# Preparing the coefficients of a long convolution: its products put behind the phase pieces, one input split over two queues, part of the scaling on ScalarE

## The chip, the cores and the metric

The kernel runs on one core of one Trainium2 chip. The metric is the device time of one execution in microseconds (us). The kernel before took 429.4 us, the median of three runs (428.68, 429.65 and 429.40). Its profile is of one further execution, which took 426.76 us.

## The reference

Two independent parts are computed and put side by side. Part A is a windowed attention (2048 tokens, 32 heads of 20, a window of 8 keys with a distance of 2). Part B is a state-space convolution over 2048 steps in 640 channels with 192 complex states for each; the change touches only its preparation:

```python
dt = jnp.exp(log_dt)[:, None]
A = A_re + 1j * A_im
Bc = B_re + 1j * B_im
Cc = C_re + 1j * C_im
logdA = dt * A
dB = dt * Bc
P = jnp.exp(logdA[:, :, None] * l[None, None, :])       # l = 0 .. 2047
K = jnp.einsum("dn,dnl,dn->dl", Cc, P, dB).real
...                                                     # y = the causal convolution of u with K, by FFT
y = y + u * Dskip[None, None, :]
return jnp.concatenate([a, b], axis=-1)
```

So three things are needed for each channel and state: the decay dt·A_re, the phase dt·A_im and the coefficient C·dt·B.

## The kernel before, in words

The 640 channels lie as 128 partitions by 5 chunks (NCH = 5). `partB_prep` loads the parameters and holds a helper `fill(c0, c1, between)`, called first for chunk 0 alone and then for chunks 1 to 4 together. For its chunks it does, in the order of its text:

- **decays** (L161 to L165): TensorE multiplies B_A_re by a diagonal of dt (tile DG) into PSUM (tile `ps_tr`) and ScalarE copies the result to `alpha`, a part of the tile LPC;
- **phase** (L182 to L194): VectorE works out dt·A_im in turns, once by itself and once times 32, each reduced to its fraction, and splits each fraction into three bf16 **pieces** hi, mid and lo (`pieces`, L168 to L174);
- **moves** (`move`, L176 to L180): twelve small DMAs carry the pieces into the tile LPC in the layout that TensorE wants, half of them issued by SyncE (SP) and half by GpSimd (POOL). The `between` of the second call also issues the loads of the tile U;
- **coefficients** (L196 to L202): for the real and the imaginary part two VectorE products p1 and p2 of B with C, their difference or sum, and one scaling by dt·4/3 for each chunk (L202), which writes the tile CN.

`B["coefficients"](c, ...)` (L204 to L211) then has TensorE transpose CN of one chunk against the constants `mix` into four PSUM tiles `ps_tr`, and ScalarE copies these to the tile cT. `psum_p` gives `ps_tr` two buffers.

`exps_chunk` (L216) lets ScalarE write powers of the decay (tile R, 45 exponentials for each chunk). `trig_half(c, h)` (L236) lets TensorE expand LPC into phases (`ps_ph`, three PSUM buffers) and ScalarE take the sine of them into the tiles TA (four activations) and TX (four activations) for one half h of a chunk; there is one buffer of TX, so the second half's TX waits until VectorE has read the first's. `small_half` (L275) is VectorE work: PG from R and TA, then Q from PG and cT, then the two X tiles from R and TX. `y_form` (L306) and `kgen_unit` (L316) form the convolution kernel from these, and everything after it (forward transform, products, inverse transform, attention) follows in `body`.

`body` (L696) writes the start in this order: chunk 0 with `fill(0, 1)`, `coefficients(0)`, constants, `exps_chunk` of chunk 0, `trig_half(0, 0)`, `fill(1, 5)`, then a loop over the chunks. The Tile framework's scheduler decides the order in which the instructions stand in each engine's queue; the engines work their queues strictly in that order. Only instructions passed through `late` (`keep_in_program_order`) are held in the order of the text, among them the DMAs. B_C_re is loaded by four DMAs on the SP queue behind the four of B_B_re; B_C_im is loaded on the POOL queue.

Some buffers matter later. The tiles of the preparation lie in the same memory that the tiles PG, Q, X and Y of the main loop use afterwards, so the first writers of those wait for the last readers of the preparation's tiles.

Of the kernel before, what the change touches and what calls it, by code (L numbers as in the profile page):

```python
# [10 lines left out]
A = mybir.AluOpType  # L11
# [83 lines left out]
def partB_prep(tc, pools, prm):  # L95
# [21 lines left out]
    def load(nm):  # L117
        nat[nm] = (pl if nm == "B_A_re" else pd).tile([128, NCH, 192], bf16, name=nm, tag=nm)
        src = prm[nm].rearrange("(g u t c) n -> u g t (c n)", g=4, u=4, t=8)
        for u in range(4):  # L120
            queue = {"B_A_re": (nc.scalar, nc.sync)[u % 2], "B_A_im": nc.gpsimd, "B_B_im": nc.gpsimd, "B_C_im": nc.gpsimd}.get(nm, nc.sync)
            late(queue.dma_start(out=nat[nm][32 * u:32 * u + 32].rearrange("p c n -> p (c n)"), in_=src[u]))

    load("B_A_re")
# [10 lines left out]
    late(nc.scalar.activation(out=dtb[:], in_=ldt[:], func=ACT.Exp))  # L135
    dtc = pl.tile([128, NCH], f32, name="dtc")
    V.tensor_copy(out=dtc[:], in_=dtb[:])
    id32 = cpool.tile([128, 32], bf16, name="id32", tag="id32")
    for u in range(4):
        V.tensor_copy(out=id32[32 * u:32 * u + 32, :], in_=ident[32 * u:32 * u + 32, 32 * u:32 * u + 32])  # L140
# [6 lines left out]
    def transposed(u, parts):  # L147

        for (o, sT, rhs, first) in parts:
            MM(o[..., 0:32], lhsT=sT[:, 0:128], rhs=rhs, start=first, stop=True, skip_group_check=True, tile_position=(32 * u, 0))  # L150
        for (o, sT, rhs, first) in parts:
            for h in range(2):
                MM(o[64 * h:64 * h + 64, ..., 32:48], lhsT=sT[:, 128:192], rhs=rhs[..., 16 * h:16 * h + 16], start=False, stop=True, skip_group_check=True, tile_position=(32 * u, 64 * h))

    def fill(c0, c1, between):
        n = c1 - c0
        cs = range(c0, c1)
        fl = lambda t: t.rearrange("p c w -> p (c w)")
        T = lambda nm, dt_, tag=None, pool=pd: pool.tile([128, n, 192], dt_, name=nm, tag=f"{tag or nm}_{n}")

        for u in range(4):  # L161
            sl = slice(32 * u, 32 * u + 32)
            ps = pspool.tile([128, NCH, UW], f32, name="ps_tr", tag="bank")
            transposed(u, [(ps[:, i], nat["B_A_re"][sl, c], DG[sl, c, :], i == 0) for i, c in enumerate(cs)])
            nc.scalar.copy(out=alpha[:, c0:c1, u, :], in_=ps[:, 0:n])  # L165
        parts = [(pd if n == 1 else ph).tile([128, 2, n * 192], bf16, name=nm, tag=f"{nm}_{n}") for nm in ("hi", "mid", "lo")]

        def pieces(b, f):  # L168
# [24 lines left out]
        pieces(0, g1)  # L193
        pieces(1, g32)  # L194
        move(between)
        for ri, (n1, n2, n3, n4, op) in enumerate((("B_B_re", "B_C_re", "B_B_im", "B_C_im", A.subtract), ("B_B_re", "B_C_im", "B_B_im", "B_C_re", A.add))):  # L196
            p1, p2 = T(f"p1{ri}", f32, "fp1"), T(f"p2{ri}", f32, "fp2")
            V.tensor_tensor(out=fl(p1), in0=fl(nat[n1][:, c0:c1]), in1=fl(nat[n2][:, c0:c1]), op=A.mult)
            V.tensor_tensor(out=fl(p2), in0=fl(nat[n3][:, c0:c1]), in1=fl(nat[n4][:, c0:c1]), op=A.mult)
            V.tensor_tensor(out=fl(p1), in0=fl(p1), in1=fl(p2), op=op)  # L200
            for i, c in enumerate(cs):
                V.tensor_scalar(out=CN[:, c, ri], in0=p1[:, i], scalar1=dtc[:, c:c + 1], scalar2=4.0 / 3.0, op0=A.mult, op1=A.mult)  # L202

    def coefficients(c, pool):  # L204
        for u in range(4):
# [4 lines left out]
                           (ps[:, 3:4], re, mix[sl, 7:8], False), (ps[:, 2:3], im, mix[sl, 8:9], False)])  # L210
            nc.scalar.copy(out=cT[:, c, u // 2, :, 12 * (u % 2):12 * (u % 2) + 12, :].rearrange("p w q f -> p w (q f)"), in_=ps[:])  # L211

    return dict(CF1=CF1, CF32=CF32, LP=LP, alpha=alpha, cT=cT, coefficients=coefficients), fill


def exps_chunk(tc, pools, B, c):  # L216
# [479 lines left out]
def body(tc, ctx, pools, prm, B_u, B_Dskip, Sd, Zd, UDd, A_x, A_wqkv, A_wo, out_a, out_b):  # L696
# [14 lines left out]
    with tc.tile_pool(name="prep_l", bufs=1) as pl, tc.tile_pool(name="prep_d", bufs=1) as pd, tc.tile_pool(name="prep_g", bufs=1) as pg, tc.tile_pool(name="prep_h", bufs=1) as ph, tc.tile_pool(name="psum_p", bufs=2, space=bass.MemoryType.PSUM) as psp:  # L711
        pools.update(prep_l=pl, prep_d=pd, prep_h=ph)
        pg.tile([128, GAP], bf16, name="gap")
        B, fill = partB_prep(tc, dict(pools, psum=psp), prm)
        fill(0, 1, lambda u: None)
        B["coefficients"](0, psp)
        Dn = pl.tile([128, 160], bf16, name="Dn")
        dsrc = B_Dskip.rearrange("(g ch) -> g ch", g=4)
        late = tc.keep_in_program_order
        late(nc.sync.dma_start(out=BD[:].rearrange("p a b n -> p (a b n)"), in_=inline(nc, cn["BD"], "c_BD")))  # L720
        late(nc.sync.dma_start(out=EA[:].rearrange("p a n -> p (a n)"), in_=inline(nc, cn["EA"], "c_EA")))
        late(nc.sync.dma_start(out=T2[:].rearrange("p a n -> p (a n)"), in_=inline(nc, cn["T2"], "c_T2")))
# [5 lines left out]
        fill(1, NCH, lambda g: late(nc.sync.dma_start(out=U[32 * g:32 * g + 32], in_=usrc[g])))  # L728
# [226 lines left out]
```

## Time and profile before

| | before |
|---|---|
| time, median of 3 runs | 429.4 us (428.68 to 429.65) |
| the profiled execution's own time | 426.76 us |
| its span in the trace | 425.0 us |
| granted TensorE clock, mean | 0.94 of full speed |
| HBM read, written | 28.08 MB, 18.35 MB |
| start of the first PG on VectorE | 31.47 us |
| start of the second half's TX on ScalarE | 41.14 us |

The span is the time from the first to the last event of the trace; what lies around it is 426.76 - 425.0 = 1.76 us. Times in a timeline are counted from the start of the span. In a timeline row stand the start, the duration of the row's instructions together, the engine, the line, the operation, what is written and read, the count, and in brackets the idle time of the engine just before and what ended it. Instructions of an engine are pipelined, so the next can start a little before the last has ended: the step from start to start is what a queue pays. PE is TensorE's matmul, PEld its weight load, DVE is VectorE, ACT is ScalarE, POOL is GpSimd and SPq is SyncE's DMA issue.

### The profile page before, as it was taken

To read this page: it belongs to the slowest core of one execution; us is meant where nothing else is said; L and a number is where in the kernel's file an instruction comes from. 1 tells how busy PE (TensorE), PEld (TensorE's weight loads), DVE (VectorE), ACT (ScalarE), POOL (GpSimd) and SP (SyncE) were. 2 spreads that over 40 slices of the span, in tenths; PEclk is the share of its full clock that TensorE was granted. 3 is DMA by queue.
4 is the path that set the end of the run, shared out by engine and by line. 5 is a ranking of instruction groups with operands and counts; after the bars stand their busy time and mean duration, and the time that the engine had idled before them with its cause. 6 is when DMAs were issued, how large, how long until landed. Compare 5 with 4: busy or idle time off the path is not lost. (4 is left out here: it accounts for less than half of the span.)

```text
span 425.0 us, 18968 instructions
## 1 busy us (share of the span) xinstructions
PE 351.9 (83%) x8693; PEld 261.5 (62%) x8693; DVE 379.0 (89%) x353; ACT 312.0 (73%) x574; POOL 39.1 (9%) x83
## 2 busy tenths in 40 slices
PE   1294769979996989969897799999799989879795
PEld 0183668867974778758785677545545666445353
DVE  7899997998997999999996989855987999999671
ACT  3984989789999999979998684433757545656552
POOL 7430000000000000000010000100000300502120
PEclk9998668999999898978997899999999999999899
DMA  5579103073233402334079942600040553887542
GB/s 148 166 174 201 25 3 126 29 244 83 102 128 127 100 29 103 143 110 102 29 274 239 217 102 93 231 2 3 2 100 2 175 114 108 239 218 203 158 127 93
DMA packets 45280, 51.76 MB, mean 122 GB/s; under 512 B 31392, under 2 KB 39136, under 8 KB 42512
## 3 DMA queue, kind: packets, MB, share of 16 engines
q1 hardware_dynamic: 41664, 41.47, 35.8%
q0 software_dynamic: 3392, 8.95, 7.2%
q8 instruction: 68, 1.11, 1.1%
q10 hardware_dynamic: 144, 0.12, 0.1%
q14 instruction: 12, 0.10, 0.1%
HBM read 28.08 MB, written 18.35 MB: 109 GB/s over the span
## 5 line engine op out<-in xcount | busy, mean ns | idle before, releaser
L312 DVE TENSOR_TENSOR Y<-PG 128x3072 bf16<-128x3072 bf16 x60 | 103.1, 1752 | 5.6 <-PE ps_k L330 5.5
L258 PE MATMUL ps_ph<-LPC 128*64 128x256 bf16 x400 | 43.7, 317 | 16.0 <-DMA LPC<-lo 8.7
L325 PE MATMUL ps_k<-Y,X 128*32 128x64 bf16 x1920 | 46.9, 239 | 8.6 <-issue 4.7
L330 PE MATMUL ps_k<-Y,X 64*32 64x64 bf16 x1920 | 44.6, 233 | 3.8 <-issue 3.8
L353 ACT CAST Sg<-ps_f 128x1024 bf16<-128x1024 f32 x40 | 37.7, 1038 | 7.7 <-PE ps_f L352 7.7
L325 PEld LDWEIGHTS <-X 128*32 128x32 bf16 x1920 | 32.2, 117 | 17.9 <-issue 9.7
L232 ACT ACTIVATE R<-LPC 128x192 bf16<-128x192 f32 x155 | 41.9, 387 | 0.0
L345 ACT CAST A<-ps_f 128x1024 bf16<-128x1024 f32 x40 | 38.0, 1045 | 2.6 <-PE ps_f L344 2.6
L330 PEld LDWEIGHTS <-X 64*32 64x32 bf16 x1920 | 30.0, 113 | 13.2 <-issue 5.3
L352 PE MATMUL ps_f<-A,T 128*64 128x128 bf16 x640 | 28.8, 265 | 10.8 <-ACT A L345 9.8
L282 DVE TENSOR_TENSOR X<-R,TX 128x1536 bf16<-128x1536 bf16 x40 | 37.2, 951 | 0.0
L258 PEld LDWEIGHTS <-LPC 128*64 128x64 bf16 x400 | 21.7, 122 | 21.7 <-issue 16.9
L266 ACT ACTIVATE TX<-ps_ph 128x768 bf16<-128x768 int16 x40 | 29.8, 837 | 6.9 <-DVE X L282 5.2
L352 PEld LDWEIGHTS <-T 128*64 128x64 bf16 x640 | 27.1, 141 | 12.4 <-issue 12.1
L618 DVE TENSOR_TENSOR prod<-v,atp 128x2048 bf16<-128x2048 bf16 (+2 forms) x32 | 30.8, 1020 | 3.5 <-PE ps_o L429 3.5
L266 ACT ACTIVATE TA<-ps_ph 128x768 bf16<-128x768 int16 x40 | 30.1, 818 | 1.4 <-PE ps_ph L262 1.4
L262 PE MATMUL ps_ph<-LPC 128*64 128x128 bf16 x400 | 29.0, 240 | 0.0
L429 PE MATMUL ps_op<-wo,o 128*128 128x320 bf16 x160 | 24.9, 307 | 1.6 <-ACT ob L430 0.9
L262 PEld LDWEIGHTS <-LPC 128*64 128x64 bf16 x400 | 24.5, 126 | 0.8
L367 DVE TENSOR_TENSOR P<-P,Sg 128x4096 bf16<-128x4096 bf16 x10 | 22.9, 2285 | 2.0 <-DMA P<-Sdram 1.6
L531 DVE TENSOR_TENSOR prod<-qT,kT 128x1024 bf16<-128x1024 bf16 (+1 forms) x16 | 23.0, 1483 | 0.5 <-ACT qT L499 0.5
L282 DVE TENSOR_TENSOR PG<-R,TA 128x3072 bf16<-128x3072 bf16 x10 | 17.5, 1752 | 6.5 <-ACT TA L266 6.5
(132 smaller groups left out, 663.9 us busy)
## 6 DMA issues: line engine op xcount, KB each, us to landing
Sdram<-Sg SPq DMA_DIRECT2D x5, 1024.0 KB
P<-Sdram SPq DMA_DIRECT2D x5, 1024.0 KB
P<-Sdram SPq DMA_DIRECT2D x10, 512.0 KB
Zdram<-Z SPq DMA_DIRECT2D x5, 1024.0 KB
Z<-Zdram SPq DMA_DIRECT2D x30, 128.0 KB
U<-in_B_u_dram SPq DMA_DIRECT2D x4, 640.0 KB
UDdram<-UD SPq DMA_DIRECT2D x10, 256.0 KB
out_dram<-ysb SPq DMA_DIRECT2D x32, 80.0 KB
```

The costliest lines, as they stand in the source:

```text
L232: nc.scalar.activation(out=RX[:, :, e - 16, :], in_=src, func=ACT.Exp, scale=m)
L258: MM(o[64 * hh:64 * hh + 64, :, 0:8], lhsT=L[:, 64 * hh:64 * hh + 64], rhs=rhs, start=first, stop=last, skip_group_check=True, tile_positi ...
L262: MM(o[64 * hh:64 * hh + 64, :, 8:12], lhsT=L[:, 128:192], rhs=rhs[:, :, 16 * hh:16 * hh + 16], start=False, stop=last, skip_group_check=T ...
L266: last = nc.scalar.activation(out=dst, in_=words.rearrange("p b (q e f) -> p b q (e f)", e=8, f=4), func=ACT.Sin, scale=PI_LO / 32768.0)
L282: TT = lambda o, a, b, op: V.tensor_tensor(out=o, in0=a, in1=b, op=op)
L312: nc.vector.tensor_tensor(out=Y[:].rearrange("p q (b a) f -> p q b a f", a=8), in0=fa, in1=gb, op=A.mult)
L325: MM(ps[32 * g:32 * g + 32, t], lhsT=X[:, q, k, :, f], rhs=Ys[k][:, q, :, f], start=(t == 0 and k == 0), stop=False, tile_position=(0, 32 ...
L330: MM(ps[32 * g:32 * g + 32, t], lhsT=X[hb, q, k, :, f], rhs=Ys[k][hb, q, :, f], start=False, stop=(k == 2), tile_position=(64 * (g // 2), ...
L345: nc.scalar.copy(out=A1[:, :, 32 * b:32 * b + 32].rearrange("p k (j g) -> p k j g", g=4), in_=ps[:].rearrange("p j k g -> p k j g"))
L352: last = MM(ps[sl, kk], lhsT=C["T2"][:, 8 * b + kk, sl], rhs=A1[:, 8 * b + kk, :], start=(kk % 4 == 0), stop=True, skip_group_check=True, ...
L353: nc.scalar.copy(out=Sg[:, :, 8 * b:8 * b + 8, :], in_=ps[:].rearrange("p k (j g) -> p j k g", g=4))
L618: ins = nc.vector.tensor_tensor(out=p2.rearrange("p (d i) -> p d i", i=ni), in0=self.v2[:, 4 * j0:4 * j0 + 4 * nj, off:off + ni], in1=at[: ...
```

## The change

- `fill` loses its first and its last part. The decays become `decays(c0, c1)`, the coefficients become `weights(c0, c1)`. `body` now calls, in this order: decays of chunk 0, `fill` of chunk 0, constants, exponentials, `trig_half(0, 0)`, `fill` of chunks 1 to 4, `weights` of chunk 0, `coefficients(0)`, decays of chunks 1 to 4, `weights` of chunks 1 to 4.
- B_C_re is loaded half on POOL (ahead of B_C_im there) and half on SP.
- A new tile `dts` holds dt·4/3, so that the scaling has one factor in place of two.
- The scaling of the real part of chunks 1 to 4 becomes four ScalarE activations (Copy with a scale); the other six scalings stay on VectorE.
- The products of the imaginary part no longer share buffers with those of the real part, but use those of the phase's tiles (tags fa and fb).

```diff
-            queue = {"B_A_re": (nc.scalar, nc.sync)[u % 2], "B_A_im": nc.gpsimd, "B_B_im": nc.gpsimd, "B_C_im": nc.gpsimd}.get(nm, nc.sync)
+            queue = {"B_A_re": (nc.scalar, nc.sync)[u % 2], "B_A_im": nc.gpsimd, "B_B_im": nc.gpsimd, "B_C_im": nc.gpsimd, "B_C_re": (nc.gpsimd, nc.sync)[u // 2]}.get(nm, nc.sync)
...
     V.tensor_copy(out=dtc[:], in_=dtb[:])
+    dts = pools["fft"].tile([128, NCH], f32, name="dts")
+    V.tensor_scalar(out=dts[:], in0=dtc[:], scalar1=4.0 / 3.0, scalar2=None, op0=A.mult)
...
+    def decays(c0, c1):
+        for u in range(4):
+            sl = slice(32 * u, 32 * u + 32)
+            ps = pspool.tile([128, NCH, UW], f32, name="ps_tr", tag="bank")
+            transposed(u, [(ps[:, i], nat["B_A_re"][sl, c], DG[sl, c, :], i == 0) for i, c in enumerate(range(c0, c1))])
+            nc.scalar.copy(out=alpha[:, c0:c1, u, :], in_=ps[:, 0:c1 - c0])
...
-        for u in range(4):
-            sl = slice(32 * u, 32 * u + 32)
-            ps = pspool.tile([128, NCH, UW], f32, name="ps_tr", tag="bank")
-            transposed(u, [(ps[:, i], nat["B_A_re"][sl, c], DG[sl, c, :], i == 0) for i, c in enumerate(cs)])
-            nc.scalar.copy(out=alpha[:, c0:c1, u, :], in_=ps[:, 0:n])
...
         move(between)
+
+    def weights(c0, c1):
+        n = c1 - c0
+        fl = lambda t: t.rearrange("p c w -> p (c w)")
+        T = lambda nm, dt_, tag: pd.tile([128, n, 192], dt_, name=nm, tag=f"{tag}_{n}")
         for ri, (n1, n2, n3, n4, op) in enumerate((("B_B_re", "B_C_re", "B_B_im", "B_C_im", A.subtract), ("B_B_re", "B_C_im", "B_B_im", "B_C_re", A.add))):
-            p1, p2 = T(f"p1{ri}", f32, "fp1"), T(f"p2{ri}", f32, "fp2")
+            p1, p2 = T(f"p1{ri}", f32, ("fp1", "fa")[ri]), T(f"p2{ri}", f32, ("fp2", "fb")[ri])
...
-            for i, c in enumerate(cs):
-                V.tensor_scalar(out=CN[:, c, ri], in0=p1[:, i], scalar1=dtc[:, c:c + 1], scalar2=4.0 / 3.0, op0=A.mult, op1=A.mult)
+            for i, c in enumerate(range(c0, c1)):
+                if n == 1 or ri == 1:
+                    V.tensor_scalar(out=CN[:, c, ri], in0=p1[:, i], scalar1=dts[:, c:c + 1], scalar2=None, op0=A.mult)
+                else:
+                    nc.scalar.activation(out=CN[:, c, ri], in_=p1[:, i], func=ACT.Copy, scale=dts[:, c:c + 1])
...
+        B["decays"](0, 1)
         fill(0, 1, lambda u: None)
-        B["coefficients"](0, psp)
...
         fill(1, NCH, lambda g: late(nc.sync.dma_start(out=U[32 * g:32 * g + 32], in_=usrc[g])))
+        B["weights"](0, 1)
+        B["coefficients"](0, psp)
+        B["decays"](1, NCH)
+        B["weights"](1, NCH)
```

In the built program the change moves instructions only in the first part of each queue; from the first PG on, VectorE's queue is the same as before.

More of the change, by code (lines that the diff above doesn't have):

```diff
@@ L211, in coefficients @@
             nc.scalar.copy(out=cT[:, c, u // 2, :, 12 * (u % 2):12 * (u % 2) + 12, :].rearrange("p w q f -> p w (q f)"), in_=ps[:])
-    return dict(CF1=CF1, CF32=CF32, LP=LP, alpha=alpha, cT=cT, coefficients=coefficients), fill
+    return dict(CF1=CF1, CF32=CF32, LP=LP, alpha=alpha, cT=cT, decays=decays, weights=weights, coefficients=coefficients), fill
 def exps_chunk(tc, pools, B, c):
```

## Prediction

> **What bounds the kernel now.** I read the page's totals first, then busy time by stage, then VectorE's waits, then the timeline of the first 42 us.
>
> ```profile
> span 425.0 us, 18968 instructions
> PE 351.9 (83%) x8693; PEld 261.5 (62%) x8693; DVE 379.0 (89%) x353; ACT 312.0 (73%) x574; POOL 39.1 (9%) x83
> ```
>
> VectorE is the fullest engine, but the change touches only the start, so the start must be read by itself. This is the windows view; its columns are the window, its length, the busy time (and count) of PE, PEld, DVE, ACT and POOL, the granted clock, the DMA share and GB/s.
>
> ```profile
> 0.00:20.00 20.00, 2.27 (x20) 1.51 (x22) 15.79 (x44) 12.67 (x48) 12.59 (x27) 1.00 0.53 141
> 20.00:31.50 11.50, 11.47 (x164) 9.63 (x162) 11.39 (x22) 9.83 (x21) 3.83 (x7) 1.00 0.79 199
> 31.50:50.00 18.50, 10.50 (x349) 8.50 (x345) 18.50 (x17) 12.53 (x30) 0.00 (x0) 0.73 0.84 134
> 50.00:74.00 24.00, 19.93 (x520) 17.36 (x522) 21.86 (x19) 22.68 (x52) 0.61 (x2) 0.78 0.15 57
> ```
>
> From 20 to 50 us VectorE is busy for 29.89 of 30 us, while ScalarE has 7.6 us free. From 50 to 74 us ScalarE is the fuller one (22.68 of 24). So VectorE sets the pace of the start, if it is also what ScalarE's stretch waits for. Among VectorE's waits only one in the preparation is over 1 us once its work has begun:
>
> ```profile
> DVE p L198 <- DMA LPC<-hi: 1.8, 1, 1.8
> ```
>
> The timeline shows where it lies and what hangs on the end of the preparation:
>
> ```profile
> 14.37 0.95 DVE L172 TENSOR_TENSOR m<-tg,hi 128x768 f32<-128x768 f32 x1
> ...
> 17.14 0.36 DVE L198 TENSOR_TENSOR p<-B_B_re,B_C_re 128x192 f32<-128x192 bf16 x1 [1.82 <-DMA LPC<-hi]
> ...
> 26.56 1.07 DVE L202 TENSOR_SCALAR CN<-p,dtc 128x192 bf16<-128x192 f32 x4
> ...
> 27.55 0.94 DVE L199 TENSOR_TENSOR p<-B_B_im,B_C_re 128x768 f32<-128x768 bf16 x1
> ...
> 31.47 1.75 DVE L282 TENSOR_TENSOR PG<-R,TA 128x3072 bf16<-128x3072 bf16 x1
> ...
> 34.01 1.75 DVE L282 TENSOR_TENSOR Q<-PG,cT 128x3072 bf16<-128x3072 bf16 x1
> ...
> 39.22 1.82 DVE L282 TENSOR_TENSOR X<-R,TX 128x1536 bf16<-128x1536 bf16 x2
> ...
> 41.14 2.92 ACT L266 ACTIVATE TX<-ps_ph 128x768 bf16<-128x768 int16 x4 [5.15 <-DVE X L282]
> ```
>
> The instruction at 17.14 reads only B_B_re and B_C_re, so it waited for the last B_C_re load; the row's "LPC<-hi" is a later load of the same queue. From there VectorE runs without a gap through the first PG (31.47) to the X tiles. ScalarE then sits idle 5.15 us until VectorE has read the single TX buffer, and starts the stretch in which it is nearly full. So there is one chain: VectorE's preparation, PG, X, ScalarE's second TX, the rest. What VectorE saves ahead of 31.47 moves all that follows, as long as nothing else comes due later.
>
> **The change, part by part.**
>
> *The stall goes.* In the new order of VectorE's queue the product of B_B_re and B_C_re stands behind lo of the first fraction of chunks 1 to 4. Rows for this and the next step:
>
> ```profile
> 7.40 1.19 POOL L122 DMA_DIRECT2D B_C_im<-in_B_C_im_dram  x2
> ...
> 9.56 2.95 SPq L122 DMA_DIRECT2D B_C_re<-in_B_C_re_dram  x4
> ...
> 10.32 0.58 POOL L179 DMA_DIRECT2D LPC<-hi  x1 [1.73 <-DVE lo L174]
> ...
> 12.63 0.72 SPq L179 DMA_DIRECT2D LPC<-hi  x1
> ...
> 13.06 0.54 DVE L171 CAST hi<-tg 128x768 bf16<-128x768 f32 x1
> ...
> 13.63 0.36 DVE L199 TENSOR_TENSOR p<-B_B_im,B_C_im 128x192 f32<-128x192 bf16 x1
> ...
> 23.37 0.55 DVE L173 CAST mid<-m 128x768 bf16<-128x768 f32 x1
> ...
> 23.84 0.95 DVE L199 TENSOR_TENSOR p<-B_B_im,B_C_im 128x768 f32<-128x768 bf16 x1
> ...
> 24.71 0.95 DVE L174 TENSOR_TENSOR lo<-m,mid 128x768 bf16<-128x768 f32 x1
> ```
>
> By the steps from start to start an instruction of 768 elements costs 0.47 with one input (23.37 to 23.84; the cast at 13.06 takes 0.57) and 0.87 with two (23.84 to 24.71). So the product comes due at 13.06 plus hi, r, m, the second fraction, mid, hi and lo, 0.57 + 0.47 + 0.87 + 0.87 + 0.47 + 0.47 + 0.87 = 4.59, at 17.7 us. Its data were there at 17.14 already with the old queues. Saved: **1.82**.
>
> *C on two queues.* SP has two issues fewer, 2 × 2.95/4 = 1.48 us, so its last B_C_re goes out by 11.0 instead of 12.5, and the piece moves behind it up to 1.5 us earlier. On POOL the two B_C_re issues (1.19 for two) push B_C_im from an end at 8.59 to 9.78; POOL was idle until 10.32, so its piece moves keep their time. B_C_im was read at 13.63 with no wait, so it lands by 13.63 + 1.19 = 14.8 now, and is due at 17.7 + 0.27 + 0.87 = 18.9, behind that product and one more difference. Value **0** for both: with the stall gone nothing waits for C.
>
> The Trainium skill speaks against this part in "SBUF — State Buffer", section "SBUF: two separate sides": a DMA issued from GpSimd needs descriptors written by GpSimd, which a VectorE instruction in a two-port mode locks out. Taken at its word the POOL half of C would land late; that is a rival below. The trace has the same kind of load on POOL in the row at 7.40, beside busy VectorE, and its reader at 13.63 did not wait.
>
> *Four scalings leave VectorE.* Four cost 1.07 us busy, and by their step (26.56 to 27.55) **0.99**. The other six keep their size.
>
> *dts is added* on 128x5 elements. The nearest row is the cast of dtc, 0.17; bounds 0 and 0.18; I take **0.17**, since VectorE has no gap behind it.
>
> ```profile
> 5.92 0.17 DVE L137 CAST dtc<-dtb 128x5 f32<-128x5 bf16 x1 [0.65 <-ACT dtb L135]
> ```
>
> Sum on VectorE: 1.82 + 0.99 - 0.17 = **2.64 us**, so PG can start at 28.83. Unknown and left at zero: the single factor in six scalings and some dependent pairs that the new order parts. The step 26.56 to 27.55 beside 0.87 for instructions of 0.95 that follow freely shows such a pair at 0.12; with three of them 0.36 more is the bound.
>
> *Does ScalarE keep up with 28.83?* Its exponentials of chunk 0 do not depend on the moved work; they end at 21.3.
>
> ```profile
> 13.88 6.42 ACT L232 ACTIVATE R<-LPC 128x192 bf16<-128x192 f32 x25
> ...
> 21.33 1.28 ACT L266 ACT_TABLE_LOAD   x1
> ...
> 22.62 0.81 ACT L266 ACTIVATE TA<-ps_ph 128x768 bf16<-128x768 int16 x1
> ...
> 23.33 0.54 ACT L211 CAST cT<-ps_tr 128x192 bf16<-128x192 f32 x2
> ...
> 25.28 0.32 ACT L211 CAST cT<-ps_tr 128x192 bf16<-128x192 f32 x1 [0.69 <-PE ps_tr L153]
> ...
> 31.07 0.56 ACT L165 COPY LPC<-ps_tr 128x192 f32<-128x192 f32 x2
> ...
> 33.76 2.22 ACT L266 ACTIVATE TA<-ps_ph 128x768 bf16<-128x768 int16 x3
> ...
> 40.96 1.75 DVE L312 TENSOR_TENSOR Y<-PG 128x3072 bf16<-128x3072 bf16 x1
> ```
>
> In the new queue the four TA and four TX activations come first, at 0.74 each (2.22/3): TA is ready at 25.6, all TX at 28.5. Then come the two copies of cT that Q needs (0.27 each): 29.1. PG is due at 28.83 and Q 2.54 later at 31.37, so ScalarE is ahead by 3.2 and 2.3 us.
>
> Ahead of the second half's TX, due at 41.14 - 2.64 = 38.5, ScalarE now has four cT copies (at most 0.32), four scalings, four decay copies (0.28) and four TA (0.74). A scaling on ScalarE is not in the trace; the nearest row is the exponential of 128x192, 6.42/25 = 0.26 a step, and the widest one, TA of 768 elements, bounds it with 0.74. I take 0.26: 1.28 + 1.04 + 1.12 + 2.96 = 6.4, so 28.5 + 6.4 = 34.9 and 3.6 us are left for waits on TensorE. The first Y now also waits for the last scaling, since it reuses p1's memory; it is due at 40.96 - 2.64 = 38.3 and the scaling stands in front of the four TA. Cost: **0**, hidden by the idle 5.15.
>
> The Trainium skill advises the other way in "ScalarE: Activation LUTs", "Rules for kernel authors": multiplication belongs on VectorE. By its formula for activations, 186 ns + 0.833 ns an element + 93 ns for a pointer operand, less 93 ns overlap, a scaling would be an estimated 0.35, four 1.4 in place of 1.04. The slack holds that too, so the sum stays by either.
>
> *The third X* has to wait until the hi pieces of chunks 1 to 4 have left the memory that it takes.
>
> ```profile
> 21.51 0.61 SPq L179 DMA_DIRECT2D LPC<-hi  x1
> ...
> 26.32 2.99 SPq L728 DMA_DIRECT2D U<-in_B_u_dram  x2
> ...
> 29.36 3.83 SPq L179 DMA_DIRECT2D LPC<-hi  x1
> ```
>
> The last of them was issued by 33.2 for an X at 39.22 that didn't wait. X comes 2.64 earlier. The queue ahead of it comes earlier too: SP reached the first hi at 21.33 and does so 1.5 earlier; lo, which U stands behind, is ready at 20.8 on VectorE instead of 25.6. So that issue moves by about 4 us, more than X does. Cost: **0**.
>
> *TensorE* has the same work. Its coefficient transposes stood between the phases and waited for VectorE there; now they stand behind three TA tiles.
>
> Sum: 426.76 - 2.64 = 424.12 us for the profiled execution (span 422.4). The median, 429.4, lies 2.64 above that execution, so the forecast for it is 429.4 - 2.64 = **426.8 us**, and by ratio the same.
>
> **The rivals.**
>
> *The clock.* The gain can shrink or grow later, where TensorE is on the path at a clock that depends on time.
>
> ```profile
> 56.00:66.00 10.00, 7.44 (x133) 7.18 (x131) 10.00 (x11) 8.85 (x19) 0.61 (x2) 0.55 0.01 2
> 66.00:74.00 8.00, 8.00 (x221) 6.39 (x221) 5.86 (x4) 7.97 (x11) 0.00 (x0) 0.93 0.43 168
> ...
> 62.63 3.63 PE L352 MATMUL ps_f<-A,T 128*64 128x128 bf16 x64 [1.57 <-ACT A L345]
> ...
> 80.25 1.53 PE L352 MATMUL ps_f<-A,T 128*64 128x128 bf16 x48
> ```
>
> The same 64 matmuls cost 3.63 at half clock and 1.53 × 64/48 = 2.04 at full clock. One such group more or less at half clock is 1.6 us: 428.4 or 425.2. "TensorE: Matmul & The Clock Gate", "What's actually happening", in the Trainium skill says the clock follows free-running windows; by that rule either may happen. For it: the clock is 0.73 and 0.78 in the windows from 31.5 to 50 and 50 to 74, and 0.55 here. Against: half clock follows idle PE there, and the whole stage shifts together.
>
> *The gain is lost at Q.* If each of the eight sine activations waits longer than 2.3/8 = 0.29 us for TensorE, cT comes late. The wait of 0.69 in the cT row, paid eight times, is 5.5 less 2.3 of slack = 3.2 late: the whole 2.64 is gone and 0.6 more. At 0.6 each, 4.8 - 2.3 = 2.5, the time is 429.3. Against: three PSUM buffers, and three TA in 2.22 without a wait.
>
> *Slower: two PSUM buffers between TensorE and ScalarE.* Eight `ps_tr` tiles (cT and decays) now go through two buffers one after another behind the sines, each possibly waiting for TensorE. With 3.6 us of slack, waits over 0.45 each eat the gain, and over (3.6 + 2.64)/8 = 0.78 each ScalarE starts its full stretch later than 41.14. At twice the 0.69 of the cT row, once for the tile and once for the one ahead of it, that is 8 × 1.38 - 6.24 = 4.8 slower: 434.2. Against: in the old order such waits were 0.3 to 0.7, and only at some.
>
> *The C wait stays.* If POOL's loads are starved, the stall comes back: it starts when they land over 18.9 - 14.8 = 4.1 us later than worked out, and at its old size of 1.82 a gain of 0.82 remains: 428.6. It is also the case in which the edit doesn't do what it says.
>
> **How the numbers follow.** Forecast 0.66, its own range 426.2 (0.36 and noise) to 427.4; clock better (425.2) 0.08, worse (428.4) 0.09; lost at Q (429.3) 0.07; slower (434.2) 0.06; C wait stays (428.6) 0.04. The range from 424.9 to 428.5 holds the first three, 0.83, with the bounds of the open costs. A measurement tells 0.2%, 0.86 us, from no change: faster is below 428.5, slower above 430.3. Faster: 0.66 + 0.08 + half of 0.09 = 0.78; same: the rest of 0.09, 0.07 and 0.04 = 0.15; slower 0.07 with a little of Q.
>
> **What would show it.** In the new profile no wait of over 0.3 us at the first product of B_B_re and B_C_re; PG at about 28.8; the second TX at about 38.5, still with idle time ended by X; the first Y without a wait for CN; C's last load before 17.7. I am wrong if PG or Q waits for ScalarE, if the second TX is ended by PE, or if PG comes at 28.8 and the stretch to 74 us gives it back.

## The result, and the profile after

The changed kernel takes 425.49 us (median of 17 runs, 422.99 to 432.35) against 428.92 for the kernel before on the same chip (17 runs). Some executions are disturbed and take longer: the ratios leave them out (two of these 17), and of e2b, e7 and g2, whose profiled execution was such a one, only rows of the first 50 us are used. The ratio, which is therefore not that of the two medians, is 0.9929, interval [0.9902, 0.9956]: 3.05 of 428.92 us less. The same kernel, run again on another chip (a2 below), gave 0.9938 [0.9907, 0.9969]. The profiled execution took 423.71 us with a span of 421.9, 3.1 below the one of before.

The page after: VectorE has lost 1.0 us of busy time and ScalarE gained 1.6.

```profile
span 421.9 us, 18968 instructions
...
PE 352.2 (83%) x8693; PEld 259.8 (62%) x8693; DVE 378.0 (90%) x350; ACT 313.6 (74%) x578; POOL 42.9 (10%) x85
```

Two of the windows of after (columns as in the prediction): from 31.5 to 50 us ScalarE is now busy for 16.65 of 18.5 us, where it was 12.53. Some 2.5 of these 4.1 us are its full stretch behind the second TX, which starts that much earlier in the window. Of the free time, which was to hide the four scalings, 1.85 us are left.

```profile
20.00:31.50 11.50, 9.56 (x129) 7.63 (x125) 11.43 (x19) 9.67 (x19) 4.70 (x6) 0.74 1.15 243
31.50:50.00 18.50, 15.66 (x501) 12.99 (x501) 18.50 (x17) 16.65 (x45) 0.00 (x0) 0.70 0.63 100
```

The timeline of after, the rows that answer to those of before:

```profile
6.26 0.17 DVE L139 TENSOR_SCALAR dts<-dtc 128x5 f32<-128x5 f32 x1
6.34 0.78 DVE L145 TENSOR_SCALAR DG<-id,dtc 128x32 bf16<-128x32 bf16 x5
...
17.69 0.34 DVE L207 TENSOR_TENSOR p<-B_B_re,B_C_re 128x192 f32<-128x192 bf16 x1
...
28.37 1.75 DVE L294 TENSOR_TENSOR PG<-R,TA 128x3072 bf16<-128x3072 bf16 x1
...
30.91 1.75 DVE L294 TENSOR_TENSOR Q<-PG,cT 128x3072 bf16<-128x3072 bf16 x1
...
36.12 1.82 DVE L294 TENSOR_TENSOR X<-R,TX 128x1536 bf16<-128x1536 bf16 x2
...
37.86 1.75 DVE L324 TENSOR_TENSOR Y<-PG 128x3072 bf16<-128x3072 bf16 x1
...
38.61 2.97 ACT L278 ACTIVATE TX<-ps_ph 128x768 bf16<-128x768 int16 x4
```

The product comes at 17.69 with no wait, and PG, Q and X come 3.10 earlier (31.47 to 28.37, 39.22 to 36.12). The second TX moves only 2.53 (41.14 to 38.61) and has lost its bracket: X had released the buffer by 37.94 (36.12 + 1.82), and ScalarE itself was late. ScalarE's own rows show why:

```profile
29.13 0.82 ACT L214 ACTIVATE CN<-p,dts 128x192 bf16<-128x192 f32 x2
31.61 0.32 ACT L223 CAST cT<-ps_tr 128x192 bf16<-128x192 f32 x1 [1.66 <-PE ps_tr L155]
32.27 0.32 ACT L223 CAST cT<-ps_tr 128x192 bf16<-128x192 f32 x1 [0.34 <-PE ps_tr L155]
...
33.58 0.32 ACT L162 COPY LPC<-ps_tr 128x192 f32<-128x192 f32 x1 [0.63 <-PE ps_tr L155]
...
35.83 2.93 ACT L278 ACTIVATE TA<-ps_ph 128x768 bf16<-128x768 int16 x4
```

Between 29.9 and 35.8 us six copies out of the two ps_tr buffers wait 3.36 us together for TensorE (the three rows shown here and three more of 0.21, 0.31 and 0.21), and two scalings take 0.82.

How far can one pair of traces be followed? These are the waits of VectorE for the third chunk's TA, and its start of the last part, in before, in after, and in the repeat of the changed kernel (a2):

```profile
130.36 1.76 DVE L282 TENSOR_TENSOR PG<-R,TA 128x3072 bf16<-128x3072 bf16 x1 [2.90 <-ACT TA L266]
...
327.29 1.23 DVE L581 TENSOR_TENSOR tree<-ql 128x1024 f32<-128x1024 f32 x1 [2.13 <-ACT ql L565]
```

```profile
128.05 1.76 DVE L294 TENSOR_TENSOR PG<-R,TA 128x3072 bf16<-128x3072 bf16 x1 [2.90 <-ACT TA L278]
...
326.36 1.23 DVE L593 TENSOR_TENSOR tree<-ql 128x1024 f32<-128x1024 f32 x1 [2.13 <-ACT ql L577]
```

```profile
128.01 1.76 DVE L294 TENSOR_TENSOR PG<-R,TA 128x3072 bf16<-128x3072 bf16 x1 [2.90 <-ACT TA L278]
...
328.56 1.22 DVE L593 TENSOR_TENSOR tree<-ql 128x1024 f32<-128x1024 f32 x1 [2.13 <-ACT ql L577]
```

At 128 us after and a2, one and the same kernel, agree within 0.04 us, 2.3 ahead of before. (At the second TX a2 was 0.70 ahead of after, 37.91 against 38.61, so that much was lost on the way.) Behind that they part by 2.2 us (326.36 and 328.56), and after's last 95.5 us (421.9 - 326.36) are 98.1 in a2 (426.7 - 328.56). So traces show where the lead comes from up to about 130 us; whether it reaches the end only the many timed runs can tell. Read naively, the pair before and after would say that the lead falls to 0.9 at 327 us and is won back at the end.

### The profile page after: what moved, and what is told of

The parts are those of the page before. It is cut to its first block, busy times and chain, and to the rows that moved or that the text cites. A ratio compares the mean times of both kernels' runs of the same rounds, so it can differ in the third digit from the quotient of the medians.

```text
span 421.9 us, 18968 instructions
## 1 busy us (share of the span) xinstructions
PE 352.2 (83%) x8693; PEld 259.8 (62%) x8693; DVE 378.0 (90%) x350; ACT 313.6 (74%) x578; POOL 42.9 (10%) x85
## 3 DMA queue, kind: packets, MB, share of 16 engines
q8 instruction: 68, 1.11, 1.1%
## 5 line engine op out<-in xcount | busy, mean ns | idle before, releaser
L337 PEld LDWEIGHTS <-X 128*32 128x32 bf16 x1920 | 32.2, 117 | 20.0 <-issue 12.5
L364 PE MATMUL ps_f<-A,T 128*64 128x128 bf16 x640 | 25.3, 244 | 12.5 <-ACT A L357 10.5
L270 PEld LDWEIGHTS <-LPC 128*64 128x64 bf16 x400 | 21.5, 121 | 19.8 <-DMA LPC<-hi 8.8
L364 PEld LDWEIGHTS <-T 128*64 128x64 bf16 x640 | 23.6, 127 | 14.3 <-issue 14.1
L630 DVE TENSOR_TENSOR prod<-v,atp 128x2048 bf16<-128x2048 bf16 (+2 forms) x32 | 30.8, 1018 | 0.7 <-PE ps_o L441 0.7
L274 PE MATMUL ps_ph<-LPC 128*64 128x128 bf16 x400 | 30.7, 249 | 0.0
L274 PEld LDWEIGHTS <-LPC 128*64 128x64 bf16 x400 | 25.8, 131 | 1.1
L441 PE MATMUL ps_op<-wo,o 128*128 128x320 bf16 x160 | 23.9, 299 | 1.8 <-ACT ysb L442 0.9
```

What stands on the lines that cost most here:

```text
L270: MM(o[64 * hh:64 * hh + 64, :, 0:8], lhsT=L[:, 64 * hh:64 * hh + 64], rhs=rhs, start=first, stop=last, skip_group_check=True, tile_positi ...
L274: MM(o[64 * hh:64 * hh + 64, :, 8:12], lhsT=L[:, 128:192], rhs=rhs[:, :, 16 * hh:16 * hh + 16], start=False, stop=last, skip_group_check=T ...
L337: MM(ps[32 * g:32 * g + 32, t], lhsT=X[:, q, k, :, f], rhs=Ys[k][:, q, :, f], start=(t == 0 and k == 0), stop=False, tile_position=(0, 32 ...
L364: last = MM(ps[sl, kk], lhsT=C["T2"][:, 8 * b + kk, sl], rhs=A1[:, 8 * b + kk, :], start=(kk % 4 == 0), stop=True, skip_group_check=True, ...
L630: ins = nc.vector.tensor_tensor(out=p2.rearrange("p (d i) -> p d i", i=ni), in0=self.v2[:, 4 * j0:4 * j0 + 4 * nj, off:off + ni], in1=at[: ...
```

## The experiments

**Theory:** there is one chain (VectorE's preparation, PG, X, second TX), and what comes earlier at the second TX is carried to the end one for one. **Rival 1:** the lead is eaten up by ScalarE and TensorE in the chunks. **Rival 2:** VectorE's PG sets the pace whatever ScalarE does. All ratios are to the kernel before on the same chip.

**e1_order_only.** The changed kernel with only its new order and the imaginary products' own buffers, without its other parts.

```diff
-            queue = {"B_A_re": (nc.scalar, nc.sync)[u % 2], "B_A_im": nc.gpsimd, "B_B_im": nc.gpsimd, "B_C_im": nc.gpsimd, "B_C_re": (nc.gpsimd, nc.sync)[u // 2]}.get(nm, nc.sync)
+            queue = {"B_A_re": (nc.scalar, nc.sync)[u % 2], "B_A_im": nc.gpsimd, "B_B_im": nc.gpsimd, "B_C_im": nc.gpsimd}.get(nm, nc.sync)
...
-                if n == 1 or ri == 1:
-                    V.tensor_scalar(out=CN[:, c, ri], in0=p1[:, i], scalar1=dts[:, c:c + 1], scalar2=None, op0=A.mult)
-                else:
-                    nc.scalar.activation(out=CN[:, c, ri], in_=p1[:, i], func=ACT.Copy, scale=dts[:, c:c + 1])
+                V.tensor_scalar(out=CN[:, c, ri], in0=p1[:, i], scalar1=dtc[:, c:c + 1], scalar2=4.0 / 3.0, op0=A.mult, op1=A.mult)
```

> The kernel after with B_C_re on one queue and all scalings on VectorE with their two factors: only the new order is left. Theory (the end follows VectorE's start, and the stall of 1.82 us is taken away by the order alone): the first PG starts at 29.3 to 29.7 us (31.47 less 1.82, less up to 0.4 for dependent pairs that the order parts), no wait of VectorE for C, time 1.8 to 2.2 us below before. Rival (the loads on two queues remove the stall): the wait stays at over 1 us, PG at 30.5 or later, time within 1 us of before. Rival (the gain comes from later stages or the clock): PG moves as said and the time does not.

Measured: 427.01 us (10 runs), ratio 0.9966 [0.9924, 1.0009]. In its timeline PG came 1.95 earlier than before, the second TX 1.94:

```profile
29.52 1.75 DVE L289 TENSOR_TENSOR PG<-R,TA 128x3072 bf16<-128x3072 bf16 x1
...
39.20 2.92 ACT L273 ACTIVATE TX<-ps_ph 128x768 bf16<-128x768 int16 x4 [4.90 <-DVE X L289]
```

ScalarE stands idle 4.90 us ahead of it, as in before. The new order moves the chain by the stall and 0.13. The time doesn't show it by itself: 1.5 us less than before (0.0034 of 428.92) where 1.8 to 2.2 were expected, with an interval that holds 1.

**e2_act_only.** The kernel before with dts and the four scalings on ScalarE, in the old order and with the old shared buffers.

```diff
-                V.tensor_scalar(out=CN[:, c, ri], in0=p1[:, i], scalar1=dtc[:, c:c + 1], scalar2=4.0 / 3.0, op0=A.mult, op1=A.mult)
+                if n == 1 or ri == 1:
+                    V.tensor_scalar(out=CN[:, c, ri], in0=p1[:, i], scalar1=dts[:, c:c + 1], scalar2=None, op0=A.mult)
+                else:
+                    nc.scalar.activation(out=CN[:, c, ri], in_=p1[:, i], func=ACT.Copy, scale=dts[:, c:c + 1])
```

> The kernel before with dts and the four scalings of chunks 1 to 4's real part on ScalarE, nothing else. Theory: the stall stays (it ends when C has landed) and swallows the 0.17 of dts; PG starts 0.99 earlier, at 30.5, time 0.8 to 1.2 below before. Rival (ScalarE has no room at this place): the copies of cT or the second half's TX come later by the scalings' 1.0 to 1.6 us, PG at 30.5 but the second TX no earlier than 41.1, time as before.

Measured: 435.28 us (4 runs), ratio 1.0155 [1.0106, 1.0203], which neither expected. Its timeline:

```profile
34.01 0.96 DVE L200 TENSOR_TENSOR p<-B_B_re,B_C_im 128x768 f32<-128x768 bf16 x1 [6.74 <-ACT CN L207]
...
46.60 2.92 ACT L271 ACTIVATE TX<-ps_ph 128x768 bf16<-128x768 int16 x4 [9.82 <-DVE X L287]
```

The imaginary part's first product writes the buffer that ScalarE still has to read, and ScalarE gets to its scalings late: VectorE waits 6.74 us.

**e3_queue_only.** The kernel before with B_C_re on two queues. **e4_one_queue.** The changed kernel with B_C_re on SP alone, the reverse of this edit.

```diff
-            queue = {"B_A_re": (nc.scalar, nc.sync)[u % 2], "B_A_im": nc.gpsimd, "B_B_im": nc.gpsimd, "B_C_im": nc.gpsimd}.get(nm, nc.sync)
+            queue = {"B_A_re": (nc.scalar, nc.sync)[u % 2], "B_A_im": nc.gpsimd, "B_B_im": nc.gpsimd, "B_C_im": nc.gpsimd, "B_C_re": (nc.gpsimd, nc.sync)[u // 2]}.get(nm, nc.sync)
```

> The kernel before with B_C_re on two queues, nothing else. Theory: C lands about 1.5 us earlier (15.7 in place of 17.1), but VectorE reaches the product before the 0.87 of m now, so the stall is still about 1.5 and PG gains only 0.5 to 0.7: PG at 30.8 to 31.0, time 0.6 below before. Rival (the two queues remove the stall): wait under 0.4, PG at 29.7, time 1.7 below before. Rival (loads on POOL are starved by VectorE): C lands later than 17.1, PG at 31.5 or later.

> The kernel after with all of B_C_re on the SP queue. Theory (value 0 of the two queues once the order is changed): the first product of B_B_re and B_C_re at 17.7 without a wait, PG at 28.4 as in the kernel after, time as the kernel after, 2.6 to 3.4 below before. Rival (it needs both): a wait of up to 1 us comes back at that product and PG is as much later than 28.4.

Measured: e3 429.42 us, 1.0002 [0.9967, 1.0037]; e4 425.3 us, 0.9925 [0.9889, 0.9961], as the changed kernel. The row of e3 that waits for C:

```profile
17.15 0.36 DVE L198 TENSOR_TENSOR p<-B_B_re,B_C_re 128x192 f32<-128x192 bf16 x1 [2.94 <-DMA B_C_re<-in_B_C_re_dram]
```

C is there at 17.15, with one queue it was at 17.14. The half on POOL was issued by 7.4 us and had landed by 14.0 at the latest:

```profile
DMA to landing us min/median/max: 6.4/6.5/6.6
```

So what came at 17.15 was SP's half, though SP had issued it by 10.8 us where before it took until 12.5. The second queue saves issue time on SP and nothing at the data. The Trainium skill says so in "DMA: Bandwidth & Descriptors", "Issuing engines are not separate DMA queues": more engines save only the time to start a transfer. These two rows agree. The PG of e3 came at 32.38, 0.91 later than before and not at 30.8 to 31.0: two instructions that VectorE did ahead of this wait in before stand behind it here, so that the wait is 2.94 in place of 1.82. In e4 the product came at 18.06 without a wait and PG at 28.75, 0.38 later than in after.

**e2b_act_own_buffers.** e2 with buffers of its own for the imaginary part, as the changed kernel has them. **e2c_moves_first.** e2b with the loads of U issued behind all transfers of the pieces. The edit of e2b, and what e2c adds to it in the loop of the transfers:

```diff
-            p1, p2 = T(f"p1{ri}", f32, "fp1"), T(f"p2{ri}", f32, "fp2")
+            p1, p2 = T(f"p1{ri}", f32, ("fp1", "fa")[ri]), T(f"p2{ri}", f32, ("fp2", "fb")[ri])
```

```diff
-                between(u)
+            for u in range(4):
+                between(u)
```

> The kernel before with the four scalings of the later chunks on ScalarE, as in the run that came out slower, but the imaginary part's two products now have buffers of their own. If the 6.74 us that VectorE waited there was the shared buffer and nothing else, no VectorE instruction waits for a scaling on ScalarE, PG starts between 30.1 us (31.47 less the four scalings of 0.99 and the step of the moved clip, up to 0.4) and 30.6, and the time is 0.7 to 1.4 us below before. Rival: the scaling itself is what costs (ScalarE gets to it late, and CN comes late to somebody), then PG or the first Y still waits for ScalarE by several us and the time stays over that of before.

> The run with buffers of its own for the imaginary part (old order, four scalings on ScalarE), where the four loads of U, 640 KB each, are issued on SP behind all twelve transfers of the phase pieces instead of between them. In that run PG came at 29.92 us, but the third X of the first half stood 1.83 us until 39.58, released by the transfers of hi, mid and lo, of which SP issues the last at 34.58 to 36.47, behind two loads of U. Theory (the pieces' transfers are a floor under the third X): PG at 29.9 as there, no wait of the third X, which starts 7.75 us behind PG at 37.7, second TX at 39.4 to 39.8 instead of 41.50, time 1.2 to 1.9 us below before. Rival (the wait was for something else, ScalarE late with its copies): the third X waits again and the second TX stays over 41.

Measured: e2b 429.8 us, 1.0028 [0.9973, 1.0082]; e2c 429.45 us, 0.9989 [0.9961, 1.0017]. Timelines of VectorE and of the SP queue in e2b, then in e2c:

```profile
29.92 1.75 DVE L287 TENSOR_TENSOR PG<-R,TA 128x3072 bf16<-128x3072 bf16 x1
...
34.58 1.89 SPq L181 DMA_DIRECT2D LPC<-lo  x1
...
39.58 1.83 DVE L287 TENSOR_TENSOR X<-R,TX 128x1536 bf16<-128x1536 bf16 x2 [1.83 <-DMA LPC<-hi]
...
41.50 2.92 ACT L271 ACTIVATE TX<-ps_ph 128x768 bf16<-128x768 int16 x4 [6.45 <-DVE X L287]
```

```profile
28.34 0.72 SPq L181 DMA_DIRECT2D LPC<-lo  x1
...
30.09 1.75 DVE L288 TENSOR_TENSOR PG<-R,TA 128x3072 bf16<-128x3072 bf16 x1
...
37.84 1.82 DVE L288 TENSOR_TENSOR X<-R,TX 128x1536 bf16<-128x1536 bf16 x2
...
39.75 2.92 ACT L272 ACTIVATE TX<-ps_ph 128x768 bf16<-128x768 int16 x4 [3.99 <-DVE X L288]
```

With own buffers the 6.74 us are gone: the buffer was the cause. But PG is 1.55 earlier in e2b and the second TX is not: the third X stood until the pieces had left the memory that it takes. With SP's last piece issued at 28.34 instead of 34.58 that wait is gone and the second TX comes 1.75 earlier. So in the old order the scalings can't pay, since the pieces' transfers are a floor under X. The time of e2c agrees with its 1.39 of lead over before (41.14 to 39.75) only at the lower end of its interval; it doesn't show a gain by itself.

**e6_imag_thrice.** A dose: the changed kernel with the imaginary part of chunks 1 to 4 computed three times. **e7_none.** The opposite dose: no weights for chunks 1 to 4, in whose place GpSimd (POOL) writes a constant. The edit of e6, then that of e7:

```diff
-        for ri, (n1, n2, n3, n4, op) in enumerate((("B_B_re", "B_C_re", "B_B_im", "B_C_im", A.subtract), ("B_B_re", "B_C_im", "B_B_im", "B_C_re", A.add))):
+        sums = list(enumerate((("B_B_re", "B_C_re", "B_B_im", "B_C_im", A.subtract), ("B_B_re", "B_C_im", "B_B_im", "B_C_re", A.add))))
+        for ri, (n1, n2, n3, n4, op) in sums + (sums[1:] * 2 if n > 1 else []):
```

```diff
-        B["weights"](1, NCH)
+        nc.gpsimd.memset(B["CN"][:, 1:NCH], 0.01)
```

> The changed kernel with the imaginary part of chunks 1 to 4 computed three times over (the same values are written again): 2 x (0.87 + 0.87 + 0.99 + 0.92) = about 7.3 us more of VectorE ahead of PG. Theory (what VectorE starts earlier or later at PG is carried to the end one for one): PG about 35.7 us, second TX about 45.2, and the time about 7 us over the changed kernel, some 4 over before. Rival (the lead of the preparation is eaten up by waits for ScalarE and TensorE in the chunks, so the end moves by a third of it, 0.9 of 3.1 as the traces of before and after stand at 327 us): PG at the same 35.7, but the time only 2 to 3 us over the changed kernel, within 1 of before.

> The changed kernel without the weights of chunks 1 to 4: their coefficients are filled with a constant by GpSimd, so the output of those chunks is not the reference's. VectorE loses 6.3 us ahead of PG. Theory (one for one only as long as ScalarE has slack before the second TX, and that slack is nearly used up): PG waits for TA at about 25.7 to 26.4 us instead of 22.5, Q for cT at about 29.2, the second TX comes at 36 to 37.5, and the time is 1 to 2.3 us under the changed kernel, not 6. Rival (VectorE alone sets the start of the chunks): the second TX near 32.5 and the time 5 to 6 us under the changed kernel. Second rival (the lead is eaten up later): within 0.5 us of the changed kernel.

Measured: e6 433.17 us, 1.0098 [1.0063, 1.0134]; e7 427.71 us, 0.9962 [0.9928, 0.9996]. Timelines of e6, then of e7:

```profile
35.63 1.75 DVE L295 TENSOR_TENSOR PG<-R,TA 128x3072 bf16<-128x3072 bf16 x1
...
45.31 2.92 ACT L279 ACTIVATE TX<-ps_ph 128x768 bf16<-128x768 int16 x4 [6.42 <-DVE X L295]
```

```profile
25.89 1.76 DVE L294 TENSOR_TENSOR PG<-R,TA 128x3072 bf16<-128x3072 bf16 x1 [2.76 <-POOL R L237]
...
30.29 1.76 DVE L294 TENSOR_TENSOR Q<-PG,cT 128x3072 bf16<-128x3072 bf16 x1 [1.77 <-ACT cT L223]
...
36.59 1.83 DVE L294 TENSOR_TENSOR X<-R,TX 128x1536 bf16<-128x1536 bf16 x2 [1.00 <-DMA LPC<-lo]
...
38.53 2.92 ACT L278 ACTIVATE TX<-ps_ph 128x768 bf16<-128x768 int16 x4 [3.08 <-DVE X L294]
```

In e6 PG is 7.26 later than in after and the second TX 6.70; the ratio rises from 0.9929 to 1.0098, 7.2 us of 428.9, give or take 1.9 by the two intervals. Rival 1 expected 2 to 3 us and falls: lateness at the second TX is carried to the end one for one, as closely as this tells. In e7 VectorE has about 6.4 us less to do (the steps of these instructions in after) and is ready for PG 5.2 earlier, at 23.13; beside POOL's constant one of its casts took 1.68 in place of 0.55. The second TX comes at 38.53, where it was. The time is that of after or a little more; the 1 to 2.3 us that my theory expected didn't come, and rival 2 falls as well. Three waits followed each other on VectorE: PG stood until TA and the last fill on POOL, which both ended at 25.8 (the row names POOL), Q stood for cT, and X for the pieces (1.00). By taking work off VectorE alone the gain of after is therefore near its limit: VectorE lost six times what the split takes off it, and nothing followed.

**g1_bf16.** The changed kernel with the products in bf16. **g2_moves_first.** g1 with all scalings on VectorE and U behind the pieces.

```diff
-            p1, p2 = T(f"p1{ri}", f32, ("fp1", "fa")[ri]), T(f"p2{ri}", f32, ("fp2", "fb")[ri])
+            p1, p2 = T(f"p1{ri}", bf16, ("fp1", "gp1")[ri]), T(f"p2{ri}", bf16, ("fp2", "gp2")[ri])
```

(g2 has the edits of e2c and of e5 beside this one.)

> The changed kernel with the two products of each coefficient written as bf16 instead of f32 to buffers of their own, so that the difference or sum reads two bf16 operands. Theory: the sums of 0.99 us for chunks 1 to 4 and those of chunk 0 take about half or less of their time, VectorE reaches PG 1.2 to 2.5 us earlier (26 to 27.2 us), Q waits for cT at about 29.2 instead of starting at 30.91, and the time is 0.8 to 1.8 us under the changed kernel. Rival (ScalarE sets the second TX already, where its idle ahead of it was nothing in the profile of the changed kernel): PG earlier by as much, the second TX not, and the time within 0.5 us of the changed kernel.

> The changed kernel with the products in bf16, all scalings on VectorE again, and the loads of U issued behind the transfers of the pieces. Theory: PG at 26.2 to 26.7 us (25.37, when VectorE was ready in the run with bf16 products, and 0.9 for the four scalings), Q at 29.25 or up to 1 us earlier, the third X 5.3 us behind Q without a wait, at 33.5 to 34.6 instead of 35.56, second TX at 35.4 to 36.5 instead of 37.50, and the time 2 to 3 us under the changed kernel. Rival (TensorE and ScalarE set the stages behind 50 us, and an earlier second TX is lost there, as the run with bf16 products was no faster than the changed kernel though its second TX came 1.1 us earlier): the same second TX, but the time within 1 us of the changed kernel.

Measured: g1 427.66 us, 0.9928 [0.9884, 0.9972]; g2 427.22 us (6 runs), 0.9877 [0.9824, 0.9930]. Timeline of g1:

```profile
29.25 1.76 DVE L294 TENSOR_TENSOR Q<-PG,cT 128x3072 bf16<-128x3072 bf16 x1 [0.91 <-ACT cT L223]
...
35.56 1.83 DVE L294 TENSOR_TENSOR X<-R,TX 128x1536 bf16<-128x1536 bf16 x2 [1.00 <-DMA LPC<-hi]
...
37.50 2.92 ACT L278 ACTIVATE TX<-ps_ph 128x768 bf16<-128x768 int16 x4 [1.43 <-DVE X L294]
```

and of g2:

```profile
30.22 1.76 DVE L292 TENSOR_TENSOR Q<-PG,cT 128x3072 bf16<-128x3072 bf16 x1 [1.53 <-ACT cT L221]
...
35.44 1.82 DVE L292 TENSOR_TENSOR X<-R,TX 128x1536 bf16<-128x1536 bf16 x2
...
37.38 2.92 ACT L276 ACTIVATE TX<-ps_ph 128x768 bf16<-128x768 int16 x4 [1.36 <-DVE X L292]
```

In g1 Q's wait came where it was expected, but also a wait for the pieces that I had not put in. The second TX is 1.11 earlier than in after, against the rival, and the 0.8 to 1.8 us under the changed kernel that the theory wanted didn't come. In g2 the pieces no longer hold X up; cT came 1 us later and took the place of that wait, so my 35.4 to 36.5 was missed. Both are faster than before. Neither is shown to be faster than the changed kernel: g2's interval overlaps those of the changed kernel, [0.9902, 0.9956] and [0.9907, 0.9969].

**e5_all_vector.** The changed kernel without the split. **a2_changed_again.** The changed kernel itself, as the measure on that chip.

```diff
-                if n == 1 or ri == 1:
-                    V.tensor_scalar(out=CN[:, c, ri], in0=p1[:, i], scalar1=dts[:, c:c + 1], scalar2=None, op0=A.mult)
-                else:
-                    nc.scalar.activation(out=CN[:, c, ri], in_=p1[:, i], func=ACT.Copy, scale=dts[:, c:c + 1])
+                V.tensor_scalar(out=CN[:, c, ri], in0=p1[:, i], scalar1=dts[:, c:c + 1], scalar2=None, op0=A.mult)
```

> The changed kernel with all eight scalings of the later chunks on VectorE. Theory: PG 0.9 to 1.0 us later than in the changed kernel, at 29.3 to 29.5 us, the second TX 0.3 to 1.0 us later than 38.43 to 38.61, where ScalarE has 1.6 us more of slack ahead of it, and the time 0.5 to 1 us over the changed kernel. Rival (the four scalings only change places from an engine with no slack to one with none): the second TX at the same place and the time within 0.3 us of the changed kernel.

> The changed kernel once more, as the measure for the other three on this chip: 0.9902 to 0.9956 of before as it was, PG at 28.4 us, second TX between 38.4 and 38.7. If the clock of TensorE between 26 and 42 us is full here (it was half in the profile of the changed kernel), ScalarE's copies wait less, and there is idle of 2 to 3 us ahead of the second TX; if it is half again, none.

Measured: e5 426.06 us (only 6 runs, 421.95 to 428.75), 0.9864 [0.9808, 0.9920]; a2 428.3 us (12 runs), 0.9938 [0.9907, 0.9969]. Timeline of e5, then of a2:

```profile
29.41 1.75 DVE L291 TENSOR_TENSOR PG<-R,TA 128x3072 bf16<-128x3072 bf16 x1
...
39.09 2.92 ACT L275 ACTIVATE TX<-ps_ph 128x768 bf16<-128x768 int16 x4 [0.85 <-DVE X L291]
```

```profile
28.23 1.75 DVE L294 TENSOR_TENSOR PG<-R,TA 128x3072 bf16<-128x3072 bf16 x1
...
37.91 2.92 ACT L278 ACTIVATE TX<-ps_ph 128x768 bf16<-128x768 int16 x4
```

PG is 1.04 later without the split than in after, as expected. The time isn't: the theory wanted 0.5 to 1 us over the changed kernel, and e5 came out below it. Six runs that spread over 7 us are too few to call it faster, but they don't support the split's price in the sum. The second TX of a2 came at 37.91 and not between 38.4 and 38.7. Its granted clock from 26 to 42 us was 0.63 in the mean, neither full nor half, and there was no idle ahead of the second TX.

**All together.** The start of PG and of the second TX in each profiled execution, and the ratio of the timed runs:

| kernel | PG | second TX | ratio |
|---|---|---|---|
| g2 | 26.07 | 37.38 | 0.9877 |
| g1 | 25.71 | 37.50 | 0.9928 |
| a2 (the changed kernel) | 28.23 | 37.91 | 0.9938 |
| e4 | 28.75 | 38.43 | 0.9925 |
| e7 | 25.89 | 38.53 | 0.9962 |
| after | 28.37 | 38.61 | 0.9929 |
| e5 | 29.41 | 39.09 | 0.9864 |
| e1 | 29.52 | 39.20 | 0.9966 |
| e2c | 30.09 | 39.75 | 0.9989 |
| before | 31.47 | 41.14 | 1 |
| e2b | 29.92 | 41.50 | 1.0028 |
| e3 | 32.38 | 42.04 | 1.0002 |
| e6 | 35.63 | 45.31 | 1.0098 |
| e2 | 36.92 | 46.60 | 1.0155 |

A straight line through these 14 points (ratio × 428.92 us) against the second TX has a slope of 1.1 us for one and a correlation of 0.93; against PG they are 0.87 and 0.85. The widest misses of the first line are e5 (3.5 us under it) and e7 (1.3 over); without e2 and e6, the two that are late by most, its correlation is 0.77. The end follows the second TX; between 37.4 and 39.1 us the points are too rough to rank kernels.

The traces show where the roughness lies. In the eleven without e2b, e7 and g2 it takes 89.1 to 90.4 us from the second TX to the third chunk's PG at about 130 us, and 293.7 (e5) to 299.6 (g1) from there to the end of the span. So what comes earlier at the second TX is still there at that PG, to within 1.3 us, and the last part differs by 5.9 from one execution to the next. e5, with the lowest ratio, has no lead over after at that PG (128.34 against 128.05): what its profiled execution gained, it gained in the last part.

## Why the prediction was right, and where not

The forecast was 2.64 us, 426.8 of 429.4, and 3.05 was measured, with 2.64 inside the interval (1.89 to 4.20 of 428.92).

- *The stall.* Due at 17.7, came at 17.69 without a wait. Shown by e1 for the place: PG 1.95 earlier from the new order, 1.82 and 0.13. The timed runs of e1 alone don't show the gain, as said there.
- *C on two queues, 0.* Right in value (e3, e4), wrong in its working: C doesn't land earlier by SP's saved issues. So the margin at the product in after is 17.69 - 17.15 = 0.5 us, if C lands there as in e3. The rival that POOL's loads are starved by VectorE did not come: the half on POOL landed first (by 14.0 in e3) and kept nothing waiting.
- *Four scalings, 0.99.* At PG they are worth 1.04 (e5 against after). That this reaches the end, which the sum took for granted, is not shown.
- *dts, 0.17.* By the step (6.26 to 6.34) 0.08. With the pairs that the new order parts this brings 3.10 at PG; it was in the bound (2.64 + 0.36 + 0.09).
- *ScalarE's slack of 3.6: this step failed.* It took 0.26 for a scaling, which took 0.41 (0.82 for two) and 0.46 where it stood alone, and no wait for TensorE. It had ScalarE done with the four TA by 34.9; that was 36.0 in e4 (33.11 + 2.93) and 38.8 in after (35.83 + 2.93). Measured idle ahead of the second TX: 2.40 us in e4 (released there by X), none in after and a2. In a2 ScalarE was just in time, and the second TX moved as far as PG (3.23 and 3.24). In after the limit is ScalarE, and part of VectorE's lead is lost (0.57, 3.10 less 2.53). The rival with two PSUM buffers had the mechanism: 3.36 / 8 = 0.42 a copy in after. It was to eat into the gain from 0.45, and with the scalings at their measured size (0.82 + 0.46 + 0.46 for 1.04), which leaves 2.9 of the 3.6, from 0.36. In after the 0.57 lost here and the 0.46 that PG gained over the forecast nearly cancel, which is luck. The estimate of 0.35 by the Trainium skill ("ScalarE: Activation LUTs") was nearer than my 0.26: a scaling behind another added 0.36 (0.82 less 0.46). And e5 does not speak against the advice of its "Rules for kernel authors" that multiplication belongs on VectorE.
- *The third X, 0.* No wait, but by less than thought: SP was done with that hi by 30.9 (26.77 and 4.12 in after's queue) and not 4 us ahead of 33.2. In e7 and g1, where VectorE comes sooner, it is a wait of 1.00.
- *The clock and TensorE's pace.* The windows from 26 to 34 us of after, of e4 and of e5:

```profile
26.00:34.00 8.00, 8.00 (x116) 6.18 (x114) 7.93 (x12) 5.00 (x12) 0.60 (x1) 0.50 1.25 184
```

```profile
26.00:34.00 8.00, 7.05 (x151) 5.59 (x150) 7.93 (x11) 7.17 (x18) 0.98 (x1) 0.99 1.25 194
```

```profile
26.00:34.00 8.00, 8.00 (x105) 6.03 (x101) 7.93 (x13) 5.59 (x11) 0.00 (x0) 1.00 1.22 201
```

The same queue order (after, e4) had TensorE at 0.50 and at 0.99 of its clock, and ScalarE busy for 5.00 and 7.17 of the 8 us. But in e5, at 1.00, ScalarE was idle for 2.4 of them too, by its rows for TensorE. So the granted clock alone does not explain ScalarE's waits. TensorE's pace does: here are the same eight matmuls in after, in e4 and in e5.

```profile
28.36 1.06 PE L270 MATMUL ps_ph<-LPC 128*64 128x256 bf16 x8
```

```profile
28.15 0.63 PE L270 MATMUL ps_ph<-LPC 128*64 128x256 bf16 x8
```

```profile
29.28 1.06 PE L267 MATMUL ps_ph<-LPC 128*64 128x256 bf16 x8
```

In e5 they were as slow as in after, though the granted clock of the window reads 1.00; what slows them there stays open. In e1 they took 0.63 as in e4, and ScalarE was done with the four TA at 34.3 without the scalings (e1) and at 36.0 with them (e4). Where they were slow, it was done at 38.2 without (e5) and at 38.8 with them (after). By these four executions TensorE's slow pace delays ScalarE by 2.7 to 3.9 us, and the four scalings by 0.5 to 1.7. The forecast's 0.17 for the clock either way was the right kind of doubt: the two profiles of the changed kernel, 421.9 and 426.7, lie further apart (4.8 us) than its rivals 425.2 and 428.4, whatever the cause.

Open, too: whether the split is worth anything (e5 against a2: 0.9864 with six runs), and where in the stages behind 130 us an execution loses or gains its 2 us and more, since the same kernel does both.

## What to carry to other kernels

Follow the chain to the first instruction of the engine that is full in the next stage, and price a change there; a lead on the engine ahead of it counts only as far as that engine, its buffers and the transfers behind it let it through. Moving work to an engine that shows idle time needs three looks: whether it shares a buffer with the one it is moved from (6.74 us here), what is issued behind it in order, and whether the idle time is still there when the chain comes earlier. To learn what a part is worth, add a dose of known size (7.26 us gave 7.2) as well as taking work away (6.4 us gave nothing): the two differ where the next limit lies close.

## What the runs showed of the hardware that was not expected

- With a second issuing queue the data of the same four loads were complete at 17.15 us (e3), with one at 17.14 (before).
- An issue on SP can hold the queue: a transfer of one 96 KB piece behind two loads of 640 KB took 4.12 us to issue in after (3.83 in before), and the pieces of e2c, ahead of which no such load stood, 0.59 to 0.72.
- The same eight matmuls took 1.06 us at a granted clock of 0.50 (after), 1.06 at 1.00 (e5) and 0.63 at 0.99 (e4).
- A scaling of 128x192 with a factor per partition took 0.46 us alone on ScalarE, 0.82 for two in a row and 1.15 for three (e2c), so 0.35 more for each that followed; on VectorE 0.25 (1.01 for four).
- Two executions of one kernel agreed within 0.04 us at 128 us and differed by 2.2 us at 327 us and by 4.8 at the end.
